# Softmax sums of an attention-plus-MLP kernel by 128x32 column tiles, reciprocals spread by small DMAs, and the multiplication moved to GpSimd

## The chip, the cores and the metric

The kernel runs on one core of one Trainium2 chip. The metric is device time in microseconds (us) of one execution, the median of three runs. The core has five instruction streams that matter here: TensorE (PE, matmuls and the loads of their stationary operand), VectorE (DVE), ScalarE (ACT), GpSimd (POOL) and SyncE (SP), which issues most DMAs. Each works through its own instructions in order and waits on semaphores for the others.

## What is computed

```
q_n, k_n = rmsnorm(q, g_q), rmsnorm(k, g_k)            # 8 batches, 12 heads, 448 tokens, head size 64
scores = (1 / 8) * q_n @ k_n^T
attn = exp(scores - max)
attn = attn / sum(attn)                                # the sums that the change is about
x = (attn @ v), heads joined                           # 3584 tokens x 768
h = x @ w_in                                           # 768 -> 2048
out = max(0.01 * h, h) @ w_out                         # 2048 -> 768
```

## The kernel before

The attention is cut into 24 units. Unit u is four heads of one batch (`b, g = divmod(u, 3)`), so three units make a batch. The four heads lie as two by two: index a picks partitions 0 to 63 or 64 to 127, index r picks the half of the keys' or outputs' partitions. Scores are computed transposed, keys on partitions and queries along the free axis, in seven steps t of 128 x 2 x 448. After the exponential they lie in the SBUF tile `et`, 128 partitions x (7, 2, 448) in fp16: partition 64r + x holds key x of head half r.

[...] `zsum` multiplies `et` by a block of ones, 64x64 tile by 64x64 tile: 7 steps x 2 r x 2 a = 28 matmuls of 64 x 448, whose result repeats each sum on 64 partitions. `pv` does the same 28 matmuls with v in place of the ones. `zinv` then computes 1/sum on ScalarE as exp(-ln(sum)), two instructions on 128x896, and `xmul` multiplies on VectorE, two instructions on 128x448, into `xt`, the fp16 input of the first MLP matrix.

PSUM has two pools. `slot()` gives tiles of two banks, two of them in rotation (tag sT); the score steps and the sums of `zsum` use them. `aux()` gives tiles of one bank, four in rotation; `pv` (two), the maximum's broadcast `pb`, and the MLP's `hps` and `op` use them.

Everything is in an order written out by hand. The main loop runs units u = 3 to 23, each in four steps d = 0 to 3. A step issues the next score matmuls (`qk`: one score step at d = 0, two at each later d), their exponentials (`ex`), and then `fill(u, d)`. `fill` takes MLP pieces from a Python list, `queue`, and issues them so that TensorE has work while ScalarE computes exponentials. A piece is either `moe1` (six matmuls `hps`, 128x448, then the leaky ReLU `gt` on ScalarE) or half of a `moe2` tile (eight matmuls `op`, 128x384). How many pieces a step takes follows from the weights `WD` and from how far it is to the next push: at d = 1 of every third unit, `push_moe1` and `push_moe2` put the pieces of the batch just finished on the list.

At d = 0 unit u also finishes unit u-1. The order is: score step 0 of u, its maximum (`shift_max`, VectorE), `zsum_slot(u-1)` and `pv(u-1)` on TensorE, `shift_mm(u)` (one matmul `pb`, then two small VectorE instructions giving the bias `eb`), `zinv(u-1)` and the first exponential of u on ScalarE, `xmul(u-1)` on VectorE. The loads of unit u+4 follow on the SP queue, `prep_qg(u+2)` and the load of v for u+3 on GpSimd, and the squares `sq` of unit u+2 on ScalarE. At d = 2 the normalised q and k of unit u+2 go through a DMA transpose on the SP queue. After the last unit, the last batch's MLP runs alone on TensorE.

Of the kernel before, what the change touches and what calls it, by code (L numbers as in the profile page):

```python
# [18 lines left out]
def kernel(  # L19
# [11 lines left out]
    nc = tc.nc  # L31
# [27 lines left out]
    make_identity(nc, ident16)  # L59
    ones16 = cst.tile([P, D], FP16)  # L60
    nc.vector.memset(ones16, 1.0)
    onesp = cst.tile([P, P], FP16)
    nc.vector.memset(onesp, 1.0)
    eps_t = cst.tile([P, 1], FP32)
# [159 lines left out]
    def gate(u):  # L224
        nc.gpsimd.tensor_copy(gate_t, buf(u, "n16")[:, 1, NS - 1, 1, D - 1:D])
# [11 lines left out]
    def zsum_slot(u):  # L237
# [2 lines left out]
        s["zt"] = [s["zslot"][:, r] for r in range(2)]  # L240
        zsum(u)

    def zinv(u):
        s = st[u]
        s["rz"] = zpool.tile([P, 2, S], FP32, tag="rz", name="rz")
        if "zslot" in s:
            nc.scalar.activation(s["rz"], s["zslot"][:, :, 0:S], AF.Ln)  # L247
            nc.scalar.activation(s["rz"], s["rz"], AF.Exp, bias=0.0, scale=-1.0)  # L248
        else:
            for r in range(2):  # L250
                nc.scalar.activation(s["rz"][:, r], s["zt"][r][:, 0:S], AF.Ln)
                nc.scalar.activation(s["rz"][:, r], s["rz"][:, r], AF.Exp, bias=0.0, scale=-1.0)

    def pv(u, t0=0, t1=NS):
        s = st[u]
        if t0 == 0:
            s["pv"] = [aux([P, 512], FP32, "pv") for r in range(2)]
        for t in range(t0, t1):
            for r in range(2):
                for a in range(2):  # L260
                    nc.tensor.matmul(s["pv"][r][64 * a:64 * a + 64, 0:S], vts[u % NV][64 * r:64 * r + 64, a, t],  # L261
                                     s["et"][64 * r:64 * r + 64, t, a], start=(t == 0), stop=(t == NS - 1))
# [53 lines left out]
    STEPS = ((0,), (1, 2), (3, 4), (5, 6))  # L316
    debt = [0.0]

    def fill(u, d):
        total = sum(c for c, _ in queue)  # L320
        left = WD[d] + 1.0
        uu, dd = u, d
        while True:
            dd += 1
            if dd == 4:
                uu, dd = uu + 1, 0
            if uu == NU or (uu % NQ == 0 and dd == 1 and (u > 3 or uu > 3)):
                break
            left += WD[dd]
        debt[0] += total * WD[d] / left  # L330
        while queue and debt[0] >= queue[0][0] * 0.5:
            c, fn = queue.pop(0)
            fn()
            debt[0] -= c
# [10 lines left out]
    with tc.manual_schedule():  # L345
        nc.scalar.dma_start(grow[:, 0], g_q[None, :])
        nc.scalar.dma_start(grow[:, 1], g_k[None, :])
        nc.scalar.preload_act_table_set("natural_log_exp_and_others")
        load(0)
        load(1)  # L350
        load(2)
        gps = aux([P, 512], FP32, "gps")
        wbank = aux([P, 512], FP32, "warm")
        warm(32)
        nc.vector.scalar_tensor_tensor(grow[:, 0], grow[:, 0], 0.125, grow[:, 1], op0=ALU.mult, op1=ALU.mult)
        nc.tensor.matmul(gps[:, 0:D], one32, grow[:, 0], start=True, stop=True)
        warm(28)
        prep_sq(0, CA, (0,))
        prep_sq(0, CB, (0,))
        acopy(ggb, gps[:, 0:D])  # L360
        prep_sq(0, ALL, (1,))
        prep_qg(0, nc.gpsimd, CA)
        prep_qg(0, nc.gpsimd, CB)
        prep_ssq(0, CA, (0,))
        prep_ssq(0, CB, (0,))
        prep_rinv(0, (0,))
        prep_ssq(0, ALL, (1,))
        prep_rinv(0, (1,))
        prep_sq(1, ALL, (0,))
        load_v(0)  # L370
        load_v(1)
        prep_norm(0, CA, (0,))
        prep_norm(0, CB, (0,))
        prep_tr(0, 0, ((CA, acopy), (CB, acopy)))
        prep_norm(0, K0, (1,))
        prep_norm(0, K1, (1,))
        tpk = aux([P, NS, P], FP16, "tp")

        def trk(c, copy):
            for x in range(*c):  # L380
                nc.tensor.transpose(tpk[:, x, :], buf(0, "n16")[:, 1, x].rearrange("p a d -> p (a d)"), ident16)
            copy(buf(0, "qkT")[:, 1, c[0]:c[1]], tpk[:, c[0]:c[1]])

        trk(K0, vcopy)
        prep_ssq(1, ALL, (0,))
        qk(0, STEPS[0])
        prep_sq(1, ALL, (1,))
        trk(K1, acopy)
        load(3)
        gate(0)  # L390
        prep_qg(1, nc.gpsimd)
        prep_sqp(2, (1,))
        shift_max(0)
        shift_mm(0)
        load_w_in(0, 1024)
        load_v(2)

        for u in range(3):
            n = u + 1
            ex(u)  # L400
            if u == 0:
                prep_ssq(n, ALL, (1,))
            prep_rinv(n)
            if u > 0:
                zinv(u - 1)
            prep_norm(n)
            load(u + 4)
            gate(n)
            prep_qg(u + 2, nc.gpsimd)
            prep_sqp(u + 3)  # L410
            load_v(u + 3)
            if u == 0:
                load_w_in(1024, 1024)
            if u == 1:
                for f in range(2):
                    load_w_out(8 * f, 8)
            qk(u, STEPS[1])
            ex(u)
            if u > 0:
                prep_tr(n, 0, VV)  # L420
                prep_tr(n, 1, VV)
                xmul(u - 1)
            qk(u, STEPS[2])
            ex(u)
            if u == 0:
                prep_tr(n, 0, VV)
            qk(u, (5,))
            ex(u)
            if u == 0:
                prep_tr(n, 1, VV)  # L430
                qk(u, (6,))
                ex(u)
                prep_sq(2, ALL, (0,))
                score0(n)
                shift_max(n)
                shift_mm(n)
            elif u == 1:
                score0(n)
                shift_max(n)
                qk(u, (6,))  # L440
                ex(u)
                shift_mm(n)
            else:
                qk(u, (6,))
                ex(u)
            if u < 2:
                zsum_slot(u)
                pv(u)
                prep_ssq(u + 2)
            else:  # L450
                prep_ssq(u + 2)
                st[u]["zt"] = [aux([P, 512], FP32, "zt") for r in range(2)]
                zsum(u, 0, 5)
                pv(u, 0, 5)
                qk(n, STEPS[0])
                zsum(u, 5, NS)
                pv(u, 5, NS)
                zinv(u)
                shift_max(n)
                xmul(u)  # L460
                push_moe1(0)
                push_moe2(0)
                queue.pop(0)[1]()
                shift_mm(n)
                ex(n)

        for u in range(3, NU):
            for d in range(4):
                if d > 0 or u > 3:
                    qk(u, STEPS[d])  # L470
                    if d == 0:
                        shift_max(u)
                        zsum_slot(u - 1)
                        pv(u - 1)
                        shift_mm(u)
                        zinv(u - 1)
                    ex(u)
                if d == 0:
                    if u == 3:
                        prep_rinv(4)  # L480
                        prep_norm(4)
                        gate(4)
                    else:
                        xmul(u - 1)
                    if u + 4 < NU:
                        load(u + 4)
                    if u + 2 < NU:
                        prep_qg(u + 2, nc.gpsimd)
                    if u + 3 < NU:
                        load_v(u + 3)  # L490
                    if 3 < u < NU - 2:
                        prep_sq(u + 2)
                if d == 1 and u % NQ == 0 and u > 3:
                    push_moe1(u // NQ - 1)
                    push_moe2(u // NQ - 1)
                if u == 3 and d == 1:
                    for ti in range(2):
                        prep_tr(4, ti, VV)
                if u + 2 < NU:
                    if d == 1:  # L500
                        prep_ssq(u + 2)
                    if d == 2:
                        prep_rinv(u + 2)
                        prep_norm(u + 2)
                        prep_trd(u + 2)
                fill(u, d)
        zsum_slot(NU - 1)
        pv(NU - 1)
        zinv(NU - 1)
        xmul(NU - 1)  # L510
        push_moe1(B - 1)
        push_moe2(B - 1)
        while queue:
            queue.pop(0)[1]()
# [28 lines left out]
```

## Time and profile before

| | before |
|---|---|
| time, median of 3 | 450.94 us (450.39 to 452.48) |
| span of the profiled run | 448.6 us |
| TensorE busy | 427.7 us, 95% of the span |
| ScalarE busy | 311.9 us, 70% |
| VectorE busy | 205.6 us, 46% |
| GpSimd busy | 100.8 us, 22% |
| sums on TensorE (L234) | 644 matmuls of 64x448, 35.2 us |
| v on TensorE (L261) | 672 matmuls of 64x448, 37.2 us |
| reciprocals on ScalarE (L247, L248) | 23 + 23 instructions of 128x896, 916 and 949 ns each |
| multiplication on VectorE (L270) | 48 instructions of 128x448, 619 ns each |

A share of busy time is a mean over the whole span; what one stage is worth is read from that stage. Matmul ends are modelled, so a group's duration includes the pipeline, and the distance between two starts is the better measure of what a group occupies. In the profile's names, a tile of `slot()` is always called sT, whatever it holds.

### The profile page before, as it was taken

How to read it: one execution, taken by the hardware profiler on the slowest of the kernel's cores; microseconds unless marked ns; L12 is line 12 of the kernel's file. 1: busy time of each engine (PE TensorE's matmuls, PEld its weight loads, DVE VectorE, ACT ScalarE, POOL GpSimd, SP SyncE). 2: the span in 40 equal slices, each digit the busy share in tenths (PEclk: the TensorE clock that was granted, in tenths of full speed). 3: DMA queues.
4: the chain of work that ended last, by engine and by line, in shares of the span. 5: the costliest groups of instructions: out<-in, count | busy, mean ns of one | idle time of the engine just before them, and what ended most of it. 6: DMA issues, size and time to landing. Idle time of an engine off the chain costs nothing.

```text
span 448.6 us, 8910 instructions
## 1 busy us (share of the span) xinstructions
PE 427.7 (95%) x3836; PEld 221.7 (49%) x3836; DVE 205.6 (46%) x317; ACT 311.9 (70%) x445; POOL 100.8 (22%) x77
## 2 busy tenths in 40 slices
PE   7577899999999999999999999999999999999995
PEld 6234445454455544554455544554455544555563
DVE  5687654553464463563454453454454530311011
ACT  6878788867964788767964788758875687544300
POOL 5988233023023033023033033033031000000000
PEclk9689999999999999999999999999999999999999
DMA  8999995585174662574263751673432330111022
GB/s 283 233 236 249 230 184 133 144 215 98 47 180 68 184 145 45 137 179 98 82 158 89 184 123 47 156 173 82 104 64 72 82 73 0 28 46 37 0 72 71
DMA packets 62508, 54.13 MB, mean 121 GB/s; under 512 B 36868, under 2 KB 57348, under 8 KB 62468
## 3 DMA queue, kind: packets, MB, share of 16 engines
q1 hardware_dynamic: 52192, 41.76, 34.9%
q0 software_dynamic: 10272, 11.80, 17.4%
q8 instruction: 30, 0.49, 0.4%
q14 instruction: 10, 0.08, 0.0%
q10 hardware_dynamic: 4, 0.00, 0.0%
HBM read 45.61 MB, written 11.01 MB: 126 GB/s over the span
## 4 chain that ended last, share of the span: by engine, by line
PE 88%; ACT 6%; DVE 3%; DMA 1%; issue 0%; SPq 0%
PE op L291 33%; PE hps L276 32%; PE sT L175 8%; PE pv L261 6%; PE sT L234 6%; ACT et L194 4%; DMA rq<-in_q_dram 1%; DVE ssq L135 1%; PE pb L219 1%; PE tp L155 1%; DVE pm L207 1%; ACT rz L248 0%; ACT rz L247 0%; ACT gt L278 0%; PE zt L234 0%
## 5 line engine op out<-in xcount | busy, mean ns | idle before, releaser
L194 ACT ACTIVATE et<-sT,eb 128x896 f16<-128x896 f32 x166 | 159.0, 1009 | 36.0 <-PE sT L175 33.1
L276 PE MATMUL hps<-xt,win 128*128 128x448 f16 x768 | 153.5, 353 | 1.3 <-DVE xt L270 1.0
L291 PE MATMUL op<-wout,gt 128*128 128x384 f16 x896 | 153.3, 326 | 0.0
L130 POOL TENSOR_TENSOR qg<-rq,ggb 128x896 f32<-128x896 f32 (+2 forms) x25 | 64.0, 2560 | 234.1 <-DVE n L147 229.8
L291 PEld LDWEIGHTS <-gt 128*128 128x128 f16 x896 | 84.6, 98 | 63.2 <-issue 10.9
L276 PEld LDWEIGHTS <-win 128*128 128x128 f16 x768 | 72.1, 98 | 74.7 <-issue 10.4
L278 ACT ACTIVATE gt<-hps 128x448 f16<-128x448 f32 x128 | 65.6, 547 | 26.0 <-PE hps L276 25.5
L295 DVE COPY ost<-op 128x384 f32<-128x384 f32 x56 | 30.9, 556 | 90.1 <-PE op L291 90.1
L147 DVE TENSOR_TENSOR n<-qg,rinv 128x896 f16<-128x896 f32 (+2 forms) x25 | 26.5, 1063 | 81.6 <-ACT rinv L141 45.7
L175 PE MATMUL sT<-qkT 64*64 64x448 f16 x664 | 52.7, 371 | 6.8 <-ACT et L194 5.2
L135 DVE TENSOR_REDUCE ssq<-sq 128x14 f32<-128x896 f32 (+2 forms) x49 | 50.0, 1058 | 6.0 <-ACT sq L122 6.0
L247 ACT ACTIVATE rz<-sT 128x896 f32<-128x896 f32 x23 | 21.1, 916 | 38.6 <-PE sT L234 38.6
L261 PE MATMUL pv<-et,vt 64*64 64x448 f16 x672 | 37.2, 357 | 0.0
L234 PE MATMUL sT<-et,ones 64*64 64x448 f16 x644 | 35.2, 355 | 0.6 <-ACT et L194 0.5
L175 PEld LDWEIGHTS <-qkT 64*64 64x64 f16 x672 | 14.6, 105 | 41.9 <-issue 38.8
L212 DVE TENSOR_REDUCE sT<-sT 128x1 f32<-128x896 f32 x22 | 24.1, 1095 | 19.2 <-PE sT L175 19.1
L270 DVE TENSOR_TENSOR xt<-pv,rz 128x448 f16<-128x448 f32 x48 | 27.8, 619 | 4.6 <-ACT rz L248 4.1
L261 PEld LDWEIGHTS <-vt 64*64 64x64 f16 x672 | 20.8, 110 | 12.3 <-issue 1.3
L234 PEld LDWEIGHTS <-ones 64*64 64x64 f16 x672 | 20.0, 107 | 12.5 <-issue 2.8
L147 DVE TENSOR_TENSOR n<-rk,rinv 128x896 f16<-128x896 f32 (+2 forms) x25 | 26.1, 1046 | 0.0
L248 ACT ACTIVATE rz<-rz 128x896 f32<-128x896 f32 x23 | 21.8, 949 | 0.7
L122 ACT ACTIVATE sq<-rq 128x896 f32<-128x896 f32 (+2 forms) x22 | 19.8, 906 | 1.3 <-DMA rq<-in_q_dram 1.3
(49 smaller groups left out, 140.0 us busy)
## 6 DMA issues: line engine op xcount, KB each, us to landing
rq<-in_q_dram SPq DMA_DIRECT2D x24, 448.0 KB, 6.1
rk<-in_k_dram SPq DMA_DIRECT2D x24, 448.0 KB, 6.7
out_dram<-ost SPq DMA_DIRECT2D x56, 192.0 KB, 2.7
vt<-in_v_dram POOLq DMA_DIRECT2D x24, 224.0 KB, 6.3
win<-in_moe_w_in_dram POOLq DMA_DIRECT2D x8, 384.0 KB, 12.6
wout<-in_moe_w_out_dram POOLq DMA_DIRECT2D x2, 1536.0 KB, 23.6
qkT<-n SPq DMA_TRANSPOSE x19, 4.0
grow<-in_g_q_dram ACTq DMA_DIRECT2D x1, 0.2 KB
```

The costliest lines, as they stand in the source:

```text
L130: eng.tensor_tensor(buf(u, "qg")[:, :, c[0]:c[1]], raw[u][0][:, :, c[0]:c[1]], ggb[:, None, None, :].broadcast_to([P, 2, n, D]), op=ALU.mult)
L135: nc.vector.tensor_reduce(buf(u, "ssq")[:, ti, :, c[0]:c[1]], buf(u, "sq")[:, ti, :, c[0]:c[1]], axis=AXL.X, op=ALU.add)
L147: nc.vector.tensor_tensor(buf(u, "n16")[:, ti, c[0]:c[1]].rearrange("p s a d -> p a s d"), src[:, :, c[0]:c[1]], buf(u, "rinv")[:, ti, :, ...
L175: nc.tensor.matmul(banks[a][64 * r:64 * r + 64, 0:S].rearrange("p (t x) -> p t x", t=NS), kT(u, r, a, t), qT(u, r, a), start=True, stop=True)
L194: nc.scalar.activation(s["et"][:, t], sT[:, :, 0:S], AF.Exp, bias=s["eb"], scale=1.0)
L234: nc.tensor.matmul(s["zt"][r][64 * a:64 * a + 64, 0:S], ones16[64 * r:64 * r + 64], s["et"][64 * r:64 * r + 64, t, a], start=(t == 0), sto ...
L261: nc.tensor.matmul(s["pv"][r][64 * a:64 * a + 64, 0:S], vts[u % NV][64 * r:64 * r + 64, a, t], s["et"][64 * r:64 * r + 64, t, a], start=(t ...
L270: nc.vector.tensor_tensor(xts[b][:, g, r], s["pv"][r][:, 0:S], s["rz"][:, r], op=ALU.mult)
L276: nc.tensor.matmul(hps[:, 0:S], win16[:, kt // 2, kt % 2, ts(ft, P)], xt[:, kt // 2, kt % 2], start=(kt == 0), stop=(kt == KT - 1))
L278: nc.scalar.activation(gt[:, ft, ds(S * (b % 2), S)], hps[:, 0:S], AF.Prelu, bias=0.0, scale=1.0, alpha=0.01)
L291: nc.tensor.matmul(op2[:, 0:HC], gt[:, ft, ts(t, P)], wout16[:, ft, ds(HC * half, HC)], start=(ft == 0), stop=(ft == FT - 1))
L295: nc.vector.tensor_copy(ost[0][:, ds(HC * half, HC)], op2[:, 0:HC])
```

## The change

For units 4 to 22 (`narrow`) the sums are made in another shape. `zcol` multiplies `et` with `onesr`, a 128x32 block: its first 16 columns are one on the partitions of r = 0 and zero elsewhere, its last 16 the same for r = 1. One matmul thus sums both r at once over all 128 partitions, and its 32 output rows hold 16 copies of each. There are four column positions c in the output bank `zc`: two for a, and two (y) for even and odd steps t; step 6 is cut into two halves of 224 columns. That makes 12 matmuls of 448 columns and 4 of 224, 16 in all instead of 28. VectorE adds the two halves y (`zcol_sum`, a copy and an addition on 64x448), ScalarE makes the reciprocals on 64x448 (`zcol_inv`), and four DMAs on the SP queue spread them to the tile `rz` on 128 partitions.

The result of `pv` moves from two one-bank tiles to a two-bank slot (`pv_slot`). ScalarE copies it to SBUF (`pv_out`, 128x896), since GpSimd multiplies it there (`xmul_pool`, 128x896). The order on TensorE at d = 0 becomes: score step 0, `pv`, `zcol`, `pb`. The batch's MLP pieces are pushed at d = 2 of every third unit (`fed`) instead of d = 1, to give the longer way to `xt` time. Units 0 to 3 and 23 keep the old form.

```diff
@@ -59,6 +59,10 @@
     make_identity(nc, ident16)
     ones16 = cst.tile([P, D], FP16)
     nc.vector.memset(ones16, 1.0)
+    onesr = cst.tile([P, 32], FP16)
+    nc.vector.memset(onesr, 0.0)
+    for r in range(2):
+        nc.vector.memset(onesr[64 * r:64 * r + 64, 16 * r:16 * r + 16], 1.0)
     onesp = cst.tile([P, P], FP16)
     nc.vector.memset(onesp, 1.0)
     eps_t = cst.tile([P, 1], FP32)
@@ -240,6 +244,51 @@
         s["zt"] = [s["zslot"][:, r] for r in range(2)]
         zsum(u)
 
+    def zcol(u):
+        s = st[u]
+        s["zc"] = aux([P, 512], FP32, "zc")
+        for t in (0, 1, 6, 2, 3, 4, 5):
+            for a in range(2):
+                halves = ((t % 2, 0, S),) if t < NS - 1 else ((0, 0, S // 2), (1, S // 2, S))
+                for y, lo, hi in halves:
+                    c = 32 * (2 * y + a)
+                    nc.tensor.matmul(s["zc"][c:c + 32, lo:hi], onesr, s["et"][:, t, a, lo:hi],
+                                     start=(t < 2), stop=(t in (4, 5)))
+
+    def pv_slot(u):
+        s = st[u]
+        s["pslot"] = slot()
+        s["pv"] = [s["pslot"][:, r] for r in range(2)]
+        pv(u)
+
+    def pv_out(u):
+        s = st[u]
+        s["x32"] = zpool.tile([P, 2, S], FP32, tag="x32", name="x32")
+        nc.scalar.copy(s["x32"], s["pslot"][:, :, 0:S])
+
+    def zcol_sum(u):
+        s = st[u]
+        s["zs"] = zpool.tile([64, S], FP32, tag="zs", name="zs")
+        nc.vector.tensor_copy(s["zs"], s["zc"][64:128, 0:S])
+        nc.vector.tensor_tensor(s["zs"], s["zc"][0:64, 0:S], s["zs"], op=ALU.add)
+
+    def zcol_inv(u):
+        s = st[u]
+        nc.scalar.activation(s["zs"], s["zs"], AF.Ln)
+        nc.scalar.activation(s["zs"], s["zs"], AF.Exp, bias=0.0, scale=-1.0)
+        s["rz"] = zpool.tile([P, 2, S], FP32, tag="rz", name="rz")
+        for r in range(2):
+            for a in range(2):
+                src = s["zs"][32 * a + 16 * r:32 * a + 16 * r + 16, None, :]
+                nc.sync.dma_start(s["rz"][64 * a:64 * a + 64, r], src.broadcast_to([16, 4, S]))
+
+    def xmul_pool(u):
+        s = st[u]
+        b, g = divmod(u, NQ)
+        if b not in xts:
+            xts[b] = xpool.tile([P, NQ, 2, S], FP16, tag="xt", name="xt")
+        nc.gpsimd.tensor_tensor(xts[b][:, g], s["x32"], s["rz"], op=ALU.mult)
+
     def zinv(u):
         s = st[u]
         s["rz"] = zpool.tile([P, 2, S], FP32, tag="rz", name="rz")
@@ -253,7 +302,7 @@
 
     def pv(u, t0=0, t1=NS):
         s = st[u]
-        if t0 == 0:
+        if t0 == 0 and "pslot" not in s:
             s["pv"] = [aux([P, 512], FP32, "pv") for r in range(2)]
         for t in range(t0, t1):
             for r in range(2):
@@ -316,6 +365,12 @@
     STEPS = ((0,), (1, 2), (3, 4), (5, 6))
     debt = [0.0]
 
+    def narrow(u):
+        return 4 <= u < NU - 1
+
+    def fed(u, d):
+        return u % NQ == 0 and d == 2
+
     def fill(u, d):
         total = sum(c for c, _ in queue)
         left = WD[d] + 1.0
@@ -324,7 +379,7 @@
             dd += 1
             if dd == 4:
                 uu, dd = uu + 1, 0
-            if uu == NU or (uu % NQ == 0 and dd == 1 and (u > 3 or uu > 3)):
+            if uu == NU or (fed(uu, dd) and (u > 3 or uu > 3)):
                 break
             left += WD[dd]
         debt[0] += total * WD[d] / left
@@ -470,16 +525,25 @@
                     qk(u, STEPS[d])
                     if d == 0:
                         shift_max(u)
-                        zsum_slot(u - 1)
-                        pv(u - 1)
-                        shift_mm(u)
-                        zinv(u - 1)
+                        if narrow(u - 1):
+                            pv_slot(u - 1)
+                            zcol(u - 1)
+                            shift_mm(u)
+                            zcol_sum(u - 1)
+                            pv_out(u - 1)
+                        else:
+                            zsum_slot(u - 1)
+                            pv(u - 1)
+                            shift_mm(u)
+                            zinv(u - 1)
                     ex(u)
                 if d == 0:
                     if u == 3:
                         prep_rinv(4)
                         prep_norm(4)
                         gate(4)
+                    elif narrow(u - 1):
+                        zcol_inv(u - 1)
                     else:
                         xmul(u - 1)
                     if u + 4 < NU:
@@ -490,7 +554,9 @@
                         load_v(u + 3)
                     if 3 < u < NU - 2:
                         prep_sq(u + 2)
-                if d == 1 and u % NQ == 0 and u > 3:
+                if d == 1 and u > 3 and narrow(u - 1):
+                    xmul_pool(u - 1)
+                if fed(u, d) and u > 3:
                     push_moe1(u // NQ - 1)
                     push_moe2(u // NQ - 1)
                 if u == 3 and d == 1:
```

## The prediction

> **What bounds the kernel now.** I read the page's busy times first, then the chain of waits, then one unit in the timeline, then busy time by unit.
>
> ```profile
> PE 427.7 (95%) x3836; PEld 221.7 (49%) x3836; DVE 205.6 (46%) x317; ACT 311.9 (70%) x445; POOL 100.8 (22%) x77
> PE 88%; ACT 6%; DVE 3%; DMA 1%; issue 0%; SPq 0%
> PE op L291 33%; PE hps L276 32%; PE sT L175 8%; PE pv L261 6%; PE sT L234 6%; ACT et L194 4%; DMA rq<-in_q_dram 1%; DVE ssq L135 1%; PE pb L219 1%; PE tp L155 1%; DVE pm L207 1%; ACT rz L248 0%; ACT rz L247 0%; ACT gt L278 0%; PE zt L234 0%
> ```
>
> TensorE is busy 95% and makes 88% of the chain that ended last. The sums (sT L234) are 6% of the chain themselves, so a microsecond less of them is a microsecond less of time, as long as no wait grows. The timeline of unit 7 shows the stage that is rewritten:
>
> ```profile
> 108.19 0.38 PE L175 MATMUL sT<-qkT 64*64 64x448 f16 x4
> 108.41 1.49 PE L234 MATMUL sT<-et,ones 64*64 64x448 f16 x28
> 109.73 1.49 PE L261 MATMUL pv<-et,vt 64*64 64x448 f16 x28
> 109.95 0.92 ACT L247 ACTIVATE rz<-sT 128x896 f32<-128x896 f32 x1 [1.11 <-PE sT L234]
> 111.16 0.23 PE L219 MATMUL pb<-dg,onesp 128*128 128x128 f16 x1
> 111.42 0.30 DVE L220 TENSOR_REDUCE sT<-pb 128x1 f32<-128x128 f32 x1 [1.31 <-PE pb L219]
> 111.95 1.01 ACT L194 ACTIVATE et<-sT,eb 128x896 f16<-128x896 f32 x1
> 114.54 1.40 ACT L278 ACTIVATE gt<-hps 128x448 f16<-128x448 f32 x3
> ```
>
> From start to start the sums occupy 109.73 - 108.41 = 1.32 us, or 47 ns per matmul. A 128*128 matmul of the same 448 columns occupies about 191 ns (18 in 114.64 - 111.22 = 3.42 us, with the start of the next group at 114.72). So four 64*64 tiles run at once. From the start of v to `pb` are 1.43 us: 1.32 of work and 0.11 for the change of tile shape.
>
> Busy time by unit (stretch; length, PE, PEld, DVE, ACT, POOL) shows who is near TensorE:
>
> ```profile
> 125.20:143.16 17.96, 17.96 (x171) 9.65 (x165) 9.66 (x16) 10.70 (x13) 4.02 (x3) 1.00 0.60 139
> 160.12:176.41 16.29, 16.29 (x149) 7.70 (x145) 7.14 (x10) 14.81 (x24) 3.56 (x3) 1.00 0.44 100
> ```
>
> In units full of `op` (first line) ScalarE has 7 us to spare; in units full of `hps` (second line) only 1.5 us, of which about 1.1 is its wait for the sums. VectorE and GpSimd have room everywhere.
>
> **What the Trainium skill says.** "TensorEngine Tiling (Array Packing)", section Tiling Modes, lists four independent 128x32 tiles, and says that a change of tiling mode drains TensorE. The trace has no 128x32 tile; the 0.11 us before `pb` agrees with a drain. "TensorE: Matmul & The Clock Gate", section Part 3, gives three column tiles of 32 a measured 2.38x and prices n tiles at one matmul plus some 4 ns for each further tile. In this trace 64x64 tiles reach 4x in a long stream; that four column tiles, each fed by all 128 partitions, do so is not shown here. "GPSIMD Engine Reference", section 3, has an fp32 two-input operation at about twice VectorE's time; the trace agrees roughly: 2.85 us on GpSimd for L130 on 128x896, 1.07 us on VectorE for L147.
>
> **The change part by part.**
>
> 1. TensorE, sums. Removed: 1.32 us per unit. Added: 12 matmuls of 448 and 4 of 224 columns. With four at once: 3 x 0.19 + 0.095 = 0.66 us, plus one more change of shape, 0.1. Bounds: 0.76 if four overlap, 0.66 x 2 + 0.1 = 1.4 if two do, 2.65 + 0.1 = 2.75 if none does. I take 0.76, because 64*64 overlaps perfectly here and the skill lists the mode: 0.56 us saved in each of 19 units, 10.6 us.
>
> 2. ScalarE. Removed: 0.92 + 0.95. Added: a copy of 128x896, taken like L247, 0.95, and two instructions on 64x448, taken like L251 and L252, 0.53 + 0.58. The sum is 0.2 more. But the position changes. Count from the start of the sums (108.41) as T. Before, the reciprocals, the exponential and both squares end at T+6.2. After: copy at T+1.45 to 2.4; `pb` comes at T+2.2 instead of 2.75, `eb` at 2.95; exponential to 3.95; meanwhile VectorE does the copy and addition (two like L270, 0.62 each) from 2.95 to 4.2; logarithm and exponential 4.25 to 5.35; squares to 7.2. So ScalarE is a microsecond later while TensorE is half a microsecond earlier. The `gt` queued behind the squares frees `hps` banks. In units full of `hps` (7, 10, 13, 16, 19, 22; the instruction order of the changed kernel gives them 66 or 72 `hps` matmuls) the fifth `hps` needs the first `gt`, at T+7.6, and TensorE is there at about T+7.3. Then the score steps of d = 2 and 3 wait for the exponentials of d = 1 and 2, each 0.2 to 0.4. I take 0.5 us per such unit (0 to 1.2): 6 x 0.5 = 3.0 us given back. In other units the 7 us of spare time hide it.
>
> 3. The way to `xt`. Before, `xt` was ready at T+4.7. After: reciprocals at T+5.35, four DMA issues at about 0.5 us each (L301 takes 0.58 for 192 KB), the last at T+7.1. Landing: before has no copy within SBUF; the stores land 2.6 us or more after issue and q's loads of four times the size in 6.1; I take 2.3, bounds 1.8 and 3.5. That is T+9.3. Multiplication on GpSimd: 1.67 (L126, both inputs the same tile) to 2.85 (L130); I take 2.1. `xt` stands at T+11.5, between 10.6 and 13.5. Behind the waiting multiplication are GpSimd's work for unit u+3 only and behind the waiting DMAs the loads of unit u+4, three units ahead of need, so these cost nothing. Only TensorE's first `hps` of a batch waits for `xt`, at its fifth matmul. By the instruction order of the changed kernel, that is reached, with 1.3 us for eight `op` and 0.5 for eight score matmuls, at: unit 6 T+9.2 (16, 8 and 8 `op` before it), unit 12 T+10.5 (16, 16, 8), units 9, 15, 18, 21 T+11.8. Waits: 2.3 + 1.0 + 4 x 0 = 3.3 us; 0.6 in all at the early end of `xt`, 4.3 + 3.0 + 4 x 1.7 = 14 at the late end.
>
> 4. Nothing on the path: 1.24 us of VectorE multiplication become 1.24 of copy and addition; the four DMAs move as many bytes as one load of q (448 KB), when DMA engines are 30 to 66% busy; `pv` in a slot is freed by a ScalarE copy at T+2.4, as the sums' slot was by L247; `zc` is freed earlier than `pv`'s banks were. Later pushes change where pieces lie, not how many; the end after unit 23 is the same.
>
> Sum: 450.9 - 10.6 + 3.0 + 3.3 = 446.6.
>
> **The rivals.**
>
> A, all hidden: `xt` arrives early and ScalarE's backlog fits in the four banks. 450.9 - 10.6 + 0.6 = 441. For it: `fed` moved by a step, about 3 us later. Against it: ScalarE at 14.81 of 16.29 us.
>
> B, a wait takes the gain: `xt` a microsecond or more later than I take it (3.3 becomes 4 + 4 x 0.7 + 2.3 = 9) and ScalarE at its upper bound (7). 450.9 - 10.6 + 9 + 4 = 453, not faster. For it: four in-order hand-overs (ScalarE, SP, DMA, GpSimd) where there was one. Against: only six units can feel `xt`.
>
> C, the tiles don't overlap as hoped. Two at once: no saving, 0.1 x 19 = 2 lost and the waits on top, 459. None: 1.43 x 19 = 27 lost, 478. For it: no such tile in this trace, four streams of 128 partitions where 64*64 has two per partition. Against: the skill's table.
>
> **How the numbers follow.** The forecast of 446.6 with its nearby variants (443 to 449.5) has 0.53, A 0.14, B 0.18, C 0.15. Faster by over 0.5% (below 448.7): all of A and about 0.43 of the forecast's 0.53, 0.57. Within 0.5%: the forecast's tail and a third of B, 0.16. Slower: 0.27. The range from 440 to 459 holds all but most of C and a sliver below A.
>
> **What would show each step.** The group of `zc` matmuls from start to start with `pb`: 0.76 us if step 1 holds, 1.4 or 2.75 if C. TensorE idle before `hps` released by GpSimd: 2 to 3 us in unit 6, one in unit 12, next to nothing elsewhere. TensorE idle before sT or `hps` released by ScalarE: some 0.5 us in units 7, 10 and so on. The last of the four DMAs landing near T+9.3 and `xt` near T+11.5. VectorE or the DMA queue as releaser of TensorE would be a cause that I don't have.

## The result, and the profile after

The changed kernel takes 463.42 us (median of four runs, 461.82 to 466.1) where the kernel before, beside it, takes 451.27 (450.39 to 452.48). The ratio is 1.0273 (95% interval 1.0216 to 1.0331): slower by 12.3 us. The profiled execution is the slowest of the four, whose times follow their mean clock (461.82 us at 0.974, 462.63 at 0.973, 464.21 at 0.970, 466.1 at 0.967), so its profile shows more slow clock than the median has. From the page of the changed kernel, the busy times, the chain of waits and the DMA issues of the reciprocals:

```profile
PE 427.2 (92%) x3608; PEld 214.9 (46%) x3608; DVE 220.7 (48%) x320; ACT 313.8 (68%) x464; POOL 142.0 (31%) x96
...
PE 60%; ACT 14%; DVE 10%; DMA 6%; POOL 3%; issue 3%; SPq 3%; DVEq 0%; POOLq 0%
PE hps L325 24%; PE op L340 18%; PE sT L179 6%; PE sT L310 5%; ACT et L198 4%; ACT sq L126 4%; DMA rz<-zs 4%; POOL xt L290 3%; PE zc L255 3%; SPq L283 2%; DVE zs L272 2%; ACT zs L277 2%; DVE zs L273 2%; ACT zs L278 2%; PE pv L310 1%
...
rz<-zs SPq DMA_DIRECT2D x76, 112.0 KB, 3.3
```

TensorE has 228 matmuls fewer and is as long busy as before. Its share of the chain has gone from 88% to 60%, and the rest of the chain names every link of the new way: `zs` on VectorE and ScalarE, the issues on the SP queue (L283), the DMAs, `xt` on GpSimd. The waits of TensorE (total us, times, longest) say where it comes out:

```profile
PE hps L325 <- POOL xt L290: 8.9, 6, 2.8
PE sT L179 <- ACT et L198: 8.3, 14, 1.2
PE pb L223 <- DVE dg L218: 4.8, 4, 1.8
```

Six times, once for each of six batches, TensorE waits for the new `xt`: 2.82 us in unit 12, 1.2 to 1.5 in units 9, 15, 18 and 21, and 0.61 in unit 6. The timeline of unit 12 (start, duration, engine, line, number of instructions, and in brackets the idle time before and who ended it):

```profile
200.28 1.49 PE L310 MATMUL sT<-et,vt 64*64 64x448 f16 x28
...
201.71 0.85 PE L255 MATMUL zc<-et,onesr 128*32 128x448 f16 x16
...
202.49 0.23 PE L223 MATMUL pb<-dg,onesp 128*128 128x128 f16 x1
...
205.19 0.58 ACT L278 ACTIVATE zs<-zs 64x448 f32<-64x448 f32 x1
...
205.83 2.94 SPq L283 DMA_DIRECT2D rz<-zs  x4
...
206.52 0.94 ACT L126 ACTIVATE sq<-rk 128x896 f32<-128x896 f32 x1
...
210.91 0.92 PE L325 MATMUL hps<-xt,win 128*128 128x448 f16 x4
...
211.58 1.09 DVE L151 TENSOR_TENSOR n<-qg,rinv 128x896 f16<-128x896 f32 x1 [2.39 <-issue]
211.66 2.94 POOL L290 TENSOR_TENSOR xt<-x,rz 128x896 f16<-128x896 f32 x1 [9.95 <-ACT rinv L145]
212.59 2.96 DVE L151 TENSOR_TENSOR n<-rk,rinv 128x896 f16<-128x896 f32 x1
...
214.65 2.72 PE L325 MATMUL hps<-xt,win 128*128 128x448 f16 x7 [2.82 <-POOL xt L290]
```

Take T = 200.28, the start of v's matmuls. The reciprocals end at T+5.5. Four issues occupy the SP queue until T+8.5; they start 0.63 to 0.66 us apart, and the last takes 1.0. The multiplication starts at T+11.4. The trace puts its wait down to `rinv` of ScalarE, which it doesn't read. The landing of the fourth DMA isn't recorded here; in the 14 units where it is, it comes 3.4 to 4.0 us after its issue. Here that would be T+10.9 to T+11.5, so this landing is taken as what releases the multiplication. The multiplication meets the two `n` of VectorE, takes 2.94 us and ends at T+14.3. TensorE, done with the four `hps` that don't need it at T+11.55, stands 2.82 us. Then the seven `hps` that follow take 2.72 us, nearly 0.39 each, where 0.19 is their pace at full clock: here the clock is lost too. By unit (length, PE, PEld, DVE, ACT, POOL, then granted clock, DMA share, GB/s), unit 12 from maximum to maximum, less 0.12 us:

```profile
200.45:221.15 20.70, 17.43 (x141) 8.05 (x137) 10.54 (x13) 12.45 (x18) 7.78 (x5) 0.92 0.81 176
```

Before, unit 12 took 16.79 us. Below, units 5 to 22 are added up, from VectorE's maximum in unit 5 to that in unit 23, since the start before varies between profiled executions (unit 3's maximum came at 44.33 us before and at 48.48 after; no run here explains that). The sum is 307.9 us before and 318.4 after.

### The profile page after: what moved, and what is told of

Read it like the earlier page. It is cut to its first block, busy times and chain, and to the rows that moved or that the text cites. A ratio compares the mean times of both kernels' runs of the same rounds, so it can differ in the third digit from the quotient of the medians.

```text
span 464.0 us, 8691 instructions
## 1 busy us (share of the span) xinstructions
PE 427.2 (92%) x3608; PEld 214.9 (46%) x3608; DVE 220.7 (48%) x320; ACT 313.8 (68%) x464; POOL 142.0 (31%) x96
## 4 chain that ended last, share of the span: by engine, by line
PE 60%; ACT 14%; DVE 10%; DMA 6%; POOL 3%; issue 3%; SPq 3%; DVEq 0%; POOLq 0%
PE hps L325 24%; PE op L340 18%; PE sT L179 6%; PE sT L310 5%; ACT et L198 4%; ACT sq L126 4%; DMA rz<-zs 4%; POOL xt L290 3%; PE zc L255 3%; SPq L283 2%; DVE zs L272 2%; ACT zs L277 2%; DVE zs L273 2%; ACT zs L278 2%; PE pv L310 1%
## 5 line engine op out<-in xcount | busy, mean ns | idle before, releaser
L325 PE MATMUL hps<-xt,win 128*128 128x448 f16 x768 | 157.3, 356 | 10.7 <-POOL xt L290 8.9
L340 PEld LDWEIGHTS <-gt 128*128 128x128 f16 x896 | 84.4, 98 | 65.8 <-issue 12.2
L290 POOL TENSOR_TENSOR xt<-x,rz 128x896 f16<-128x896 f32 x19 | 41.1, 2162 | 214.7 <-DMA rz<-zs 159.7
L134 POOL TENSOR_TENSOR qg<-rq,ggb 128x896 f32<-128x896 f32 (+2 forms) x25 | 64.2, 2570 | 38.1 <-DVE n L151 33.7
L151 DVE TENSOR_TENSOR n<-qg,rinv 128x896 f16<-128x896 f32 (+2 forms) x25 | 35.7, 1430 | 76.6 <-POOL xt L290 28.0
L179 PE MATMUL sT<-qkT 64*64 64x448 f16 x664 | 55.2, 378 | 9.8 <-ACT et L198 8.3
L267 ACT COPY x<-sT 128x896 f32<-128x896 f32 x19 | 17.2, 906 | 33.1 <-PE sT L310 33.1
L151 DVE TENSOR_TENSOR n<-rk,rinv 128x896 f16<-128x896 f32 (+2 forms) x25 | 29.8, 1196 | 0.0
L310 PE MATMUL sT<-et,vt 64*64 64x448 f16 x532 | 28.4, 349 | 0.1
L126 ACT ACTIVATE sq<-rk 128x896 f32<-128x896 f32 x20 | 18.7, 936 | 1.3 <-DMA rk<-in_k_dram 1.3
L106 POOL DMA_DIRECT2D vt<-in_v_dram x24 | 18.3, 763 | 0.0
L255 PE MATMUL zc<-et,onesr 128*32 128x448 f16 (+1 forms) x304 | 16.1, 332 | 0.0
```

The source lines that it names most:

```text
L126: nc.scalar.activation(buf(u, "sq")[:, ti, :, c[0]:c[1]], raw[u][ti][:, :, c[0]:c[1]], AF.Square)
L134: eng.tensor_tensor(buf(u, "qg")[:, :, c[0]:c[1]], raw[u][0][:, :, c[0]:c[1]], ggb[:, None, None, :].broadcast_to([P, 2, n, D]), op=ALU.mult)
L151: nc.vector.tensor_tensor(buf(u, "n16")[:, ti, c[0]:c[1]].rearrange("p s a d -> p a s d"), src[:, :, c[0]:c[1]], buf(u, "rinv")[:, ti, :, ...
L179: nc.tensor.matmul(banks[a][64 * r:64 * r + 64, 0:S].rearrange("p (t x) -> p t x", t=NS), kT(u, r, a, t), qT(u, r, a), start=True, stop=True)
L290: nc.gpsimd.tensor_tensor(xts[b][:, g], s["x32"], s["rz"], op=ALU.mult)
L325: nc.tensor.matmul(hps[:, 0:S], win16[:, kt // 2, kt % 2, ts(ft, P)], xt[:, kt // 2, kt % 2], start=(kt == 0), stop=(kt == KT - 1))
```

## The experiments

Three causes stood against each other in the first four runs: TensorE's wait for `xt`, which is late by its own long way; the collision of `n` and `xt`, which makes `xt` and VectorE's later work late; and the push a step later, which leaves TensorE with fewer MLP pieces in the first unit of a batch. In the expectations that use letters, A is the collision and B the wait. Ratios are to the kernel before in the same series, with 95% intervals.

**The later push alone**, on the kernel before:

```diff
-                if d == 1 and u % NQ == 0 and u > 3:
+                if d == 2 and u % NQ == 0 and u > 3:
```

(and the same in `fill`'s test).

> The kernel before with one thing of the change: MLP pieces pushed at d = 2 instead of d = 1. Theory (the loss comes from the new way to xt, not from where the pieces lie): same as before within 0.5%, 451 us, no TensorE wait for xt, TensorE clock as before. Rival (the later push leaves d = 1 of units 6, 12, 18 with too few pieces, TensorE waits for exponentials there): 454 to 457 us, with TensorE idle before sT released by ScalarE.

Measured: 1.0046 (1.0032 to 1.0059), 2.1 us. Units 5 to 22 add up to 308.6 us, 0.7 more. Unit 6 has 24 `hps` and 32 `op` where it had 48 and 24, and what was not done there is done later: after the last unit's `pb` come 312 MLP matmuls instead of 304, and from the last maximum to the end it is 65.5 us instead of 64.2. TensorE waits for `xt` as little as before (1.0 us). So the push isn't free, and it is a sixth of the loss, not its cause.

**The normalisation a step earlier**, on the changed kernel, to part `n` from `xt`:

```diff
                     if d == 1:
                         prep_ssq(u + 2)
-                    if d == 2:
                         prep_rinv(u + 2)
                         prep_norm(u + 2)
                         prep_trd(u + 2)
```

> The changed kernel with the reciprocal root and the normalisation of unit u+2 (and its DMA transpose) at d = 1 instead of d = 2, so that VectorE's two n instructions are over before GpSimd multiplies. Theory A (VectorE and GpSimd shut each other out, and that is on the path): every n back at 1.09 us, every xt at 2.07 us, TensorE's waits for pb gone in the unit after, xt one us earlier; 463.4 becomes 456 to 459 us. Theory B (only the length of the way to xt counts, the four DMAs above all): 461 to 463 us.

Measured: 1.0239 (1.0203 to 1.0274). It didn't part them: now the second `n` met `xt` (on average 1577 ns, and 2342 ns for `xt`). The time, 462.15 us, lies where B had it, but the collision wasn't taken away, so the run decides nothing between the two.

**The push another step later** (`fed` at d = 3 in place of 2), and **both edits together**:

> The changed kernel with the pieces pushed at d = 3 instead of d = 2. Theory B (TensorE's wait for xt, 8.9 us with the slow clock after it, is the loss): waits for xt below 1 us, clock above 0.97, 463.4 becomes 452 to 455 us. Theory A (the collision of n and xt makes VectorE, and with it pb of the next unit, late): n still 3 us in several units, time 458 to 461 us.

> Both edits, normalisation at d = 1 and pieces pushed at d = 3. If waits for xt and the collision are together the loss in the main loop, what is left is the saving of 0.56 us in 19 units less ScalarE's delays and whatever the start lost: 444 to 449 us, faster than before. If ScalarE or the start carry much of the loss, 450 to 455 us.

Measured: 1.0017 (1.0002 to 1.0032) and 1.0022 (1.0006 to 1.0038). The same waits with the push at d = 3:

```profile
PE hps L325 <- POOL xt L290: 0.9, 1, 0.9
```

Pushing still later, which should hurt if the late push were the loss, wins back 11.5 us, because nearly all `hps` now come after their `xt`. The waits of 8.9 us in all are down to 0.9, while `n` and `xt` go on colliding (the first `n` 1310 ns on average, 1500 in the change; `xt` 2158 and 2162). With both edits they collide more (the second `n` 1906 ns, `xt` 2369), and the time is the same. So the waiting, with what it brings, is the loss. But the two edits together stay well above the 444 to 449 us of the second expectation: even without the waits, something holds the gain back.

**No reciprocals in the multiplication.** GpSimd multiplies by a constant 1/448, so the division by the sums is left out, and `xt` waits for `pv_out` alone. All other work, the four DMAs too, stays (the line that fills `rzc` isn't shown):

```diff
-        nc.gpsimd.tensor_tensor(xts[b][:, g], s["x32"], s["rz"], op=ALU.mult)
+        nc.gpsimd.tensor_tensor(xts[b][:, g], s["x32"], rzc[:, None, :].broadcast_to([P, 2, S]), op=ALU.mult)
```

> The changed kernel, but GpSimd multiplies by a constant tile instead of rz, so that the normalisation by the sums is left out for units 4 to 22; sums, reciprocals and the four DMAs are still done, but nobody waits for them. xt then stands at about T+5 (T: start of v), clear of n. If the way through the DMAs is the loss, waits for xt and long n vanish: 445 to 449 us. If ScalarE's later order or DMA traffic carries a large part, 452 us or more.

Measured: 0.996 (0.9944 to 0.9976), 450.28 us, outside what was expected on the high side. Against the changed kernel that is 0.0313 x 451 = 14.1 us: the price of the late `xt` with all that comes with it, the waits, the collision (every `n` takes 1.09 us now, every `xt` 2.08) and the slow clock. Unit 12, in the same columns as above:

```profile
192.54:208.63 16.09, 15.64 (x145) 7.70 (x141) 8.66 (x14) 12.47 (x18) 6.06 (x4) 1.00 0.83 178
```

16.09 us instead of 20.70, at full clock. The loss lies in the units that need `xt`: 3.3 us in 5 and 6 together, 1.5 in 9, 4.6 in 12, 1.4 in 15, 1.7 in 17 and 18, 1.65 in 21; that is all 14.1. TensorE no longer waits for `xt` at all, and yet only 1.8 us of the gain on the sums (0.004 x 451) are left. So something else takes the rest.

**ScalarE's order.** The same, with the two instructions for the reciprocals behind the exponentials of d = 1 instead of ahead of them:

```diff
-                    elif narrow(u - 1):
-                        zcol_inv(u - 1)
-                    else:
+                    elif not narrow(u - 1):
                         xmul(u - 1)
...
                 if d == 1 and u > 3 and narrow(u - 1):
+                    zcol_inv(u - 1)
```

> e7_const (normalisation by the sums left out for units 4 to 22) with the two reciprocal instructions on ScalarE at d = 1 behind the exponentials instead of d = 0 ahead of the squares. Theory (ScalarE's later order costs some 0.5 us in every unit full of hps and in those with a thin d = 1, 5.9 us in all by a comparison of unit lengths): 450.3 becomes 445 to 447 us. Rival (that loss comes from DMA traffic, the copy of pv or the slot it holds, which all stay): 449 to 451 us.

Measured: 0.9835 (0.9807 to 0.9863), 444.57 us, just below what was expected. So the order on ScalarE costs 0.0125 x 451 = 5.6 us. By unit, 1.7 us of it are in 7, 10, 13, 16 and 19 (0.2 to 0.4 each), and 3.5 in 5, 6, 11, 12 and 17 (0.35, 1.5, 0.5, 0.65 and 0.5), which work off the end of a batch's pieces. In 5, 6 and 12 TensorE waits for exponentials (0.45, 1.17 with 0.51, and 0.45 us; none above 0.3 us is left there afterwards); in 11 and 17 the 24 `op` of d = 1 take 4.58 us instead of 4.08, since in unit 11 the `gt` ahead of them ends 1.5 us later. TensorE's longest group of waits in both (first without, then with the edit; the constant shifts the line numbers by two):

```profile
PE sT L181 <- ACT et L200: 8.3, 14, 1.2
```

```profile
PE sT L181 <- ACT et L200: 6.0, 11, 1.1
```

With the push alone, units 5 to 22 took 308.6 us; here they take 299.1, each 0.45 to 0.55 us less. That is the whole saving of the narrow sums. The copy of `pv`, its slot and the DMA traffic are all still there, so they cost TensorE next to nothing.

**Half of the DMAs issued by GpSimd**, on the changed kernel:

```diff
-                nc.sync.dma_start(s["rz"][64 * a:64 * a + 64, r], src.broadcast_to([16, 4, S]))
+                (nc.sync, nc.gpsimd)[r].dma_start(s["rz"][64 * a:64 * a + 64, r], src.broadcast_to([16, 4, S]))
```

> The changed kernel with two of the four DMAs issued by GpSimd, which is idle there, and two by SP. If the four issues one after another on SP (3.0 us) are a large part of the way to xt: xt starts about 1.2 us sooner, each of the six waits shorter by that, 463.4 becomes 456 to 460 us. If the landing time rules, or GpSimd's own DMAs land later: 462 to 465 us.

Measured: 1.0153 (1.0114 to 1.0192), 5 us better than the change. The waits for `xt` are 6.9 us in place of 8.9; that of unit 12 is 1.35 in place of 2.82, the unit takes 17.60 us, and its clock stays full. The four issues one after the other are part of the lateness, less than expected: in the six units with a wait `xt` starts 0.1 to 0.7 us sooner and not 1.2, since each DMA then lands 3.7 (SP) or 3.9 us (GpSimd) after its issue. In unit 12 `xt` also escapes the collision (2.06 us in place of 2.94).

**The old form where `xt` is needed at once.** The last unit of each batch keeps the old sums and `xmul`, the push goes back to d = 1:

```diff
-        return 4 <= u < NU - 1
+        return 4 <= u < NU - 1 and u % NQ < NQ - 1
...
-        return u % NQ == 0 and d == 2
+        return u % NQ == 0 and d == 1
```

> The changed kernel, but the last unit of every batch keeps the old sums (zsum, reciprocals on ScalarE, multiplication on VectorE), and the pieces are pushed at d = 1 as before. 13 units use the new form. If the loss is TensorE's wait for the last xt of a batch and the later push, what stays is 13 x 0.54 = 7.0 us saved, less some ScalarE delay in units full of hps: 445 to 448 us, faster than before by about 1%. If the new form itself costs as much as it saves (ScalarE order, collision of n and xt, DMA traffic): 450 to 453 us.

Measured: 0.9906 (0.9873 to 0.9939), 446.94 us: faster than both kernels. Thirteen units keep the narrow sums, and none of them is waited for.

**And the reciprocals late.** In addition the reciprocals behind the exponentials of d = 1, and the multiplication at d = 3 (they leave d = 0 as in the run on ScalarE's order, which isn't shown again):

```diff
-                    xmul_pool(u - 1)
+                    zcol_inv(u - 1)
+                if d == 3 and u > 3 and narrow(u - 1):
+                    xmul_pool(u - 1)
```

> Like e5_lastold, and for the 13 units the reciprocals are made at d = 1, behind the exponentials, and GpSimd multiplies at d = 3. This takes two ScalarE instructions (1.15 us) out of the stretch before the squares and moves xt behind n. If ScalarE's order and the collision cost in e5_lastold: one to three us faster than it, 443 to 446 us, n back at 1.09 us each. If they cost nothing: the same as e5_lastold.

Measured: 0.9866 (0.9838 to 0.9894), 445.23 us, the best version with the whole computation. Saving 0.54 us (below) in 13 units makes 7.0 us; 0.0134 x 451 = 6.0 arrive. Its interval overlaps that of the run before; the next run settles the step by unit.

**Is it the collision?** In the last version `n` and `xt` also no longer meet, so its gain over the one before it could be that. On the version with the old form at the batch's end, one small copy that waits for `n`, ahead of each multiplication, parts them and leaves the reciprocals where they were (the multiplication's old place at d = 1 goes):

```diff
+                if d == 2 and u > 3 and narrow(u - 1):
+                    if u + 2 < NU:
+                        gate(u + 2)
+                    xmul_pool(u - 1)
```

> e5_lastold with one small GpSimd copy of an element of n (0.18 us, the one that gate makes elsewhere) ahead of each multiplication, so that GpSimd multiplies only when VectorE's two n instructions are over; ScalarE's order and the DMAs stay as in e5_lastold. Every n must be back at 1.09 us and every xt at 2.07 us. If the collision costs time where nobody waits for xt: 445 to 446 us. If it costs none there and only ScalarE's order parts e5_lastold from e6_lazy: 446.5 to 447.5 us, with units 7, 10, 13, 16 as long as in e5_lastold (16.67, 16.26, 17.61, 16.27 us).

Measured: 0.9909 (0.9884 to 0.9935), no different from 0.9906. The groups of `n` and `xt`, without the copy and then with it (count | busy us, mean ns | idle before, and what ended it):

```profile
L290 POOL TENSOR_TENSOR xt<-x,rz 128x896 f16<-128x896 f32 x13 | 27.8, 2140 | 155.9 <-DMA rz<-zs 126.1 <-ACT gt L327 20.2 <-ACT rinv L145 9.6
L151 DVE TENSOR_TENSOR n<-qg,rinv 128x896 f16<-128x896 f32 x23 | 27.2, 1181 | 79.3 <-ACT rinv L145 36.4 <-POOL xt L290 21.7 <-issue 21.2
```

```profile
L290 POOL TENSOR_TENSOR xt<-x,rz 128x896 f16<-128x896 f32 x13 | 27.0, 2079 | 42.5 <-DMA rz<-zs 42.1
L151 DVE TENSOR_TENSOR n<-qg,rinv 128x896 f16<-128x896 f32 x23 | 25.1, 1092 | 79.2 <-issue 42.8 <-ACT rinv L145 36.4
```

The copy parts them (`n` no longer waits for `xt`), and units 7, 10, 13 and 16 take 16.67, 16.26, 17.61 and 16.25 us, as without it to 0.02. With the reciprocals late they take 16.25, 15.84, 17.29 and 15.85. Over units 5 to 22 it is 304.7 us without the copy, 304.5 with it, and 302.2 with the reciprocals late; 2.0 of these last 2.3 us are in 7, 10, 13, 16 and 19. So the step from 0.9906 to 0.9866 is mostly ScalarE's order again. The collision moves about a microsecond from a unit to the next (5 and 6, 17 and 18) but costs only 0.3 us in all where nobody waits for `xt`.

**The DMAs at the end of d = 2**, another try at parting them: the four DMAs in a function of their own, `spread`, called behind the transpose of unit u+2 (the old place of the multiplication goes, and `spread` itself isn't shown).

```diff
+                if d == 2 and u > 3 and narrow(u - 1):
+                    spread(u - 1)
+                    xmul_pool(u - 1)
```

> e5_lastold with the reciprocals still at d = 0 on ScalarE, but the four DMAs issued at the end of d = 2, so that GpSimd multiplies after n is over and nothing else changes. If the collision of n and xt costs where nobody waits for xt (n late, pb of the next unit late): 445 to 446 us, as e6_lazy. If only ScalarE's order made the difference between e5_lastold and e6_lazy: 446.5 to 447.5 us, although every n is back at 1.09 us.

Measured: 1.0102 (1.0062 to 1.0141), 455.55 us, slower than both expectations. Every `n` is back at 1.09 us, but something else changed. The timeline of unit 9 shows why:

```profile
146.77 1.57 SPq L163 DMA_TRANSPOSE qkT<-n  x1
...
148.44 4.04 SPq L286 DMA_DIRECT2D rz<-zs  x4
...
156.14 2.07 POOL L293 TENSOR_TENSOR xt<-x,rz 128x896 f16<-128x896 f32 x1 [12.11 <-DMA rz<-zs]
...
158.26 2.05 PE L328 MATMUL hps<-xt,win 128*128 128x448 f16 x10 [0.76 <-POOL xt L293]
```

The DMAs stand on the SP queue behind the transpose, which waits for `n`. They go out in the next unit, and `xt` of the batch's second group is late now: TensorE waits 6.5 us for it in four places, with units 6, 12 and 18 at 21.88, 20.90 and 20.65 us. The same wait for `xt`, made in another way, costs as it does in the change.

**VectorE multiplies**, in the best version, at d = 0 of the unit after the next, instead of GpSimd (the calls that move it there aren't shown):

```diff
-        nc.gpsimd.tensor_tensor(xts[b][:, g], s["x32"], s["rz"], op=ALU.mult)
+        nc.vector.tensor_tensor(xts[b][:, g], s["x32"], s["rz"], op=ALU.mult)
```

> e6_lazy with the multiplication on VectorE, one unit later at d = 0, instead of GpSimd. If VectorE has the room that its busy share shows: the same as e6_lazy, 444.5 to 446 us, and GpSimd was never needed. If a further 1.1 us on VectorE ahead of the sums of squares makes later work late: 447 us or more.

Measured: 0.9905 (0.9881 to 0.9929), 447.05 us, in the range for later work that comes late. It isn't late in the units: from unit 4 to 23 they take the same as with GpSimd to 0.04 us (318.41 and 318.45). It is late at the end. From the last maximum on it is 65.2 us instead of 63.9, because unit 22's multiplication now stands behind all of unit 23's on VectorE, and TensorE waits for it:

```profile
401.14 7.16 PE L325 MATMUL hps<-xt,win 128*128 128x448 f16 x37 [1.08 <-DVE xt L290]
```

The profiled spans (445.1 and 445.4) hide this, since the starts differ by 1.5 us the other way. So within the units GpSimd isn't needed: VectorE has the room. At the end this placing costs 1.3 us; another place for unit 22's multiplication wasn't tried.

## Why the prediction was wrong

Over units 5 to 22 the parts add up: 18 x 0.54 = 9.7 us saved on the sums, 0.7 for the later push, 5.2 for ScalarE's order (304.3 to 299.1 us in the pair that measured it), 14.1 for the late `xt`. That makes +10.3 us; measured are 318.4 - 307.9 = +10.5. Over the whole, the push's tail adds 1.1 (1.3 in the run with the push alone).

- **Step 1, the sums: right.** From the start of v to `pb` the timeline has 202.49 - 200.28 = 2.21 us, before 111.16 - 108.41 = 2.75: 0.54 saved, taken as 0.56. From the start of `zc` to `pb` 0.78 us, taken as 0.76. Rival C is out.
- **Step 2, ScalarE: mechanism right, size and place off.** "6 x 0.5 = 3.0 us given back" measured 5.6. The units named gave 1.7 (0.2 to 0.4 each, none in 22). "In other units the 7 us of spare time hide it" was the fault: that holds in the units with 80 `op` (8, 14, 20), which gave nothing, but units 5, 6, 11, 12 and 17 gave 3.5. There TensorE waits for exponentials, or its `op` wait for `gt`. Few MLP pieces alone don't mark such a unit: 9 and 15 have 66 matmuls, about as many as 12, and gave nothing.
- **Step 3, the way to `xt`: this step failed.** It put `xt` at T+11.5 and the waits at 3.3 us; the runs give `xt` at T+13.4 to T+14.6 (T+14.3 in unit 12), waits of 8.9 us, and 14.1 us with what comes with them. Term by term: the reciprocals at T+5.5 (taken 5.35) are right. The four issues take 2.94 us, while "the last at T+7.1" allows 1.75 (four at "about 0.5" would end at T+7.35, a slip, as is T+9.3 for 7.1 + 2.3), so the last ends at T+8.5. From there to the start of the multiplication are 2.9 us, where 2.3 were taken for the landing. That makes T+11.4 in place of T+9.3. The multiplication takes 2.07 alone, as taken, but 2.94 when it meets `n`, which wasn't thought of. The 2.85 us of L130, read as the price of GpSimd, was this collision already: in the kernel before, the same instruction takes 2.07 where no `n` runs (last section). The late end (13.5, "14 at the late end") was near the truth, and was given little weight.

  The 14.1 isn't TensorE's waiting for `xt` alone (8.9). The clock halves twice, in units 6 and 12, for 3.41 us each (last section), which costs up to half of that, 1.7 us, each time; in unit 12 a wait of 2.82 us goes with 4.6 us. And `pb` of unit 6 waits 1.17 us for VectorE, made late by the collision in unit 5, a wait that is gone without the reciprocals. These make up to 13.5 of the 14.1; the rest wasn't traced.

  That only the first `hps` of each of six batches feel `xt` was as said; where the waits are longest was not. Unit 6, put at 2.3 us, waited 0.61, because TensorE, itself held up, came to its fifth `hps` at T+14.0 and not T+9.2. Unit 12, put at 1.0, waited 2.82. Units 9, 15, 18 and 21, put at 0, waited 1.2 to 1.5 (TensorE at T+12.2 to T+12.4, `xt` at T+13.4 to T+13.7) and lost 1.4 to 1.7.
- **Step 4, "Nothing on the path": wrong by 2.1 us.** "Later pushes change where pieces lie, not how many; the end after unit 23 is the same": the first run shows 1.3 us of MLP work moved to the tail, where nothing hides it, and 0.7 in the units. No wait of TensorE is put down to VectorE's copy and addition. But VectorE does release TensorE late once, in the wait of `pb` just named, "a cause that I don't have".
- **"VectorE and GpSimd have room everywhere"** holds by busy time (48% and 31% in the page), and it hid that the two get into each other's way. Where `xt` isn't awaited that costs 0.3 us (the copy's run). In unit 12 it lengthens `xt` by 0.87 us of the 2.82 waited. No run takes the collision alone out of the change, so what it costs there in time stays open.

Rival B, "a wait takes the gain", is what happened, with its own late `xt`. That its waits, 9 us, come to the measured 8.9 is luck, as the single ones differ. Its sum of 453 counts 4 for ScalarE where its words say 7 (that would be 456; measured 5.2 to 5.6). It was still too low, since it priced the wait as TensorE's idle time and had nothing for the clock, the collision and the push.

## What to carry to other kernels

Add up an in-order chain of hand-overs with the late end of every term, and ask where the consumer stands at that moment. If it is TensorE, allow for a slow clock after waits of some microseconds too: here the waits were 8.9 of a loss of 14.1. A saving that is spread over all units can be taken only where its result isn't needed at once: keep the short path in the unit that is awaited, and put the new work behind the instructions that TensorE waits for. "Spare time" of an engine holds for the stage in which it was read; ask for it in every kind of stage, above all where the filler runs low. And before a duration is taken as the price of an instruction, look at what ran beside it.

## What the runs showed of the hardware

- **`n` on VectorE and `xt` or `qg` on GpSimd wait each other out.** `n` takes 1.09 us alone, `xt` and `qg` 2.07. In unit 12 above they start at 211.58, 211.66 and 212.59 and take 1.09, 2.94 and 2.96: the first `n` keeps its time, `xt` is longer by 0.87 us of the 1.01 that it overlaps with it, and the second `n` by 1.87 of 2.01. The wait shows as a longer instruction and not as idle time. In unit 5 the same, and then `qg`, which overlaps with the second `n` by 0.99 us and takes 2.93:

```profile
91.29 1.09 DVE L151 TENSOR_TENSOR n<-qg,rinv 128x896 f16<-128x896 f32 x1 [2.39 <-issue]
91.36 2.97 POOL L290 TENSOR_TENSOR xt<-x,rz 128x896 f16<-128x896 f32 x1 [9.38 <-ACT rinv L145]
92.30 2.98 DVE L151 TENSOR_TENSOR n<-rk,rinv 128x896 f16<-128x896 f32 x1
94.29 2.93 POOL L134 TENSOR_TENSOR qg<-rq,ggb 128x896 f32<-128x896 f32 x1
```

  The kernel before has it too, 18 times: `qg` at 17.67 runs beside no `n`, that at 104.34 beside one.

```profile
17.67 2.07 POOL L130 TENSOR_TENSOR qg<-rq,ggb 128x896 f32<-128x896 f32 x1
104.17 1.08 DVE L147 TENSOR_TENSOR n<-rk,rinv 128x896 f16<-128x896 f32 x1
104.34 2.85 POOL L130 TENSOR_TENSOR qg<-rq,ggb 128x896 f32<-128x896 f32 x1 [11.85 <-DVE n L147]
```

  The Trainium skill, "GPSIMD Engine Reference", section Specifications, says that GpSimd shares its SBUF interfaces with VectorE and contends with instructions that have two SBUF inputs. These two have them, and the trace agrees; its numbers fit waiting out the other instruction, not both slowing down. In the run with the constant, `xt` overlaps VectorE's copy and addition of the sums, which read PSUM, and keeps its 2.08 us.
- **TensorE's clock halved for 3.41 us at a time.** In the trace of the change this comes twice in the units. The stretch before and the stretch itself, in unit 6 and in unit 12 (columns as above, the clock third from the end):

```profile
102.10:105.51 3.41, 1.73 (x15) 0.83 (x14) 1.71 (x2) 3.41 (x5) 0.00 (x0) 1.00 0.88 134
105.51:108.92 3.41, 2.80 (x10) 1.16 (x8) 2.25 (x1) 1.04 (x3) 2.06 (x1) 0.50 0.80 276
211.33:214.74 3.41, 0.59 (x4) 0.25 (x3) 3.16 (x2) 0.16 (x1) 3.08 (x2) 1.00 0.89 319
214.74:218.15 3.41, 3.41 (x16) 1.10 (x15) 1.28 (x2) 0.91 (x2) 3.41 (x2) 0.50 0.45 93
```

  Unit 12's follows the wait of 2.82 us for `xt`. Unit 6's follows two waits for exponentials (1.17 and 0.51 us) and begins before its wait for `xt`. "TensorE: Matmul & The Clock Gate", section Part 1, gives half rate after an idle window of some 3.4 us; here TensorE was busy for 0.59 and 1.73 us of the 3.41 ahead. In the run with the DMAs behind the transpose, waits of 2.2 and 2.3 us went with a clock of 0.92 in units 6 and 12. With half the DMAs on GpSimd a wait of 1.73 us in unit 6 went with a full clock, and so did the same two waits for exponentials in the run with the constant. So no length of wait that decides comes out of these runs.
- **Small copies within SBUF are not quick.** 112 KB, made of 16 rows written four times each, land 3.3 us after issue (median), and four of them on one queue take 2.94 us to issue.
- **128x32 tiles overlap four times.** 12 matmuls of 448 and 4 of 224 columns take 0.78 us from the first start to the next shape's first, the change of shape included, where one after the other at 0.19 and 0.095 they would take 2.66.
